# Attention with a small memory, then a gated feed-forward layer: side work at fixed half steps, two output rows fetched in advance, and a last pass that adds on GpSimd and stores on two queues

## The chip, the cores and the metric

The kernel runs on one core of one Trainium2 chip. The metric is the device time of one execution in microseconds. The engines are TensorE (PE, with its weight loads PEld), VectorE (DVE), ScalarE (ACT), GpSimd (POOL) and SyncE (SP); the last three also issue the kernel's DMA transfers.

## The reference, cut to what matters

```python
# attention: B=8, H=8, S=576, D=64, a memory of M=32 slots
a = softmax(phi, axis=2)                            # phi: B,H,S,M
k_m = einsum('bhsm,bhsd->bhmd', a, k)               # keys of the memory
v_m = einsum('bhsm,bhsd->bhmd', a, v)               # values of the memory
attn = softmax(q @ k_m.T / 8)                       # B,H,S,M
x = (attn @ v_m).transpose(0, 2, 1, 3).reshape(4608, 512)
# feed-forward: 512 -> 1536 -> 512
out = (sigmoid(x @ w_gate) * (x @ w_val)) @ w_out
```

## The kernel before

All products are made of a high and a low part in fp32r (hi, lo), three products for each. A batch's attention weights stand turned in at_hi and at_lo. Instead of x, the kernel multiplies the memory's values with the gate's and the value's weights (u_hi, u_lo, made by make_u), so a gate is at times U into pu_t; ScalarE takes the sigmoid of one half (sg or x), VectorE multiplies (L826, L1001), and the parts of the product (g, g_hi, g_lo) go against the output weights into acc.

The program has four stretches. An opening list, written out by hand, ends at about 170 us and is not touched. The **main loop** (to about 391 us) works through batches 0 to 3, four of the twelve blocks of 128 gate columns at a time (TURN): a step is one block, it has two half steps, and after each four steps a batch's sums go to DRAM (part) or, for the last four, to the output. The **second loop** works through batches 4 to 7 with twelve passes (s = 0 to 11) for each batch, where `seven` makes seven products of sums of columns in place of eight (ring holds the weights; acc takes them), and `merge` adds them up into two rows of 128x512. Then comes the tail: the last `seven`, the last `merge`, and the stores.

Beside both loops runs the side work for the batches to come. For phi: its maximum nmx (`a_max`, L420), exp (`a_exp`, which writes ph and its sum z), the turning (T0 to T2), and sums (`memory`). For the scores: `scores`, their maximum (`s_max`, `s_minus`), exp in place in e (`s_exp`), `normalize`, and `turn` into at_hi. Exp and sigmoid need different tables on ScalarE, so an ACT_TABLE_LOAD stands on either side of a stretch of exps. Side work is handed out piece by piece:

```python
            beside = chain(kept_keys(b + 1), softmax(b + 1, then), attend(b + 1), turns_of(then) if then else ())
            slots = iter([1] + [0] * 8 + [1, 0, 1, 0, 1, 0, 1, 0, 1, 1, 1, 1])
```

`go_on` runs once in each half step and takes as many pieces as slots says. Each engine works off its instructions in order. The order of TensorE's products, of the sigmoids and exps, and of the DMA issues of one queue is that of the code; the rest is placed by a scheduler, which may pull an instruction forward. `behind()` holds what is in it back behind the last sigmoid, product, u and conversion that were written before it. The maxima, exps and turns of phi are outside of it before the change.

At the end of four steps `out_end` adds acc to the earlier sum in row (L871) and stores it. `row_of` takes one of two buffers named row and fetches the earlier sum on ScalarE's queue ("rows"); other queues are "batch" on SyncE and "stream" on GpSimd. A batch has four such rows of 128x512. Rows 0 and 1 are fetched when the second half of a step comes to its end, rows 2 and 3 when the first two are stored, since they use the same two buffers. Six rooms named left, of the same size, hold what is left over of gates (the last 64 rows of a batch) until `out_left` works it off.

Of the kernel before, what the change touches and what calls it, by code (L numbers as in the profile page):

```python
# [2 lines left out]

# [17 lines left out]
P = 128  # L21
# [20 lines left out]
DONE = 20  # L42
NBLK = 2
PAIRS = NFT // 2 // NBLK
LEFT_AT = [(1, 2), (0, 0)]
AHEAD = {(1, 0): 2, (0, 1): 2}
SEVEN = [(0, 3, 0), (1, 0, 0), (5, 0, 1), (4, 1, 0), (3, 1, 1), (2, 2, 0), (6, 2, 1)]


# [64 lines left out]
def attn_moe_kernel(  # L114
# [510 lines left out]
    def s_max(b, c=None):  # L625

        e = blocks(b, c)
        w = e.shape[2]
        mx = note("mx")[:, :, :w]
        nc.vector.tensor_reduce(mx, e, axis=AX.X, op=ALU.max)  # L630
        loaded[b, "mx", c] = mx
# [132 lines left out]
        for i, f in enumerate(fs):  # L764
            U[b, f] = (hi[:, :, i], lo[:, :, i])

    left = {}

    def left_of(pair, f):

# [57 lines left out]
    def gate_hi(b, f, c):  # L828
        prod = G[b, f, c][1]
        g = g_tile()  # L830
        ghi, glo = g[:, :, 0], g[:, :, 1]
        nc.scalar.copy(ghi, prod[:, : 2 * P].rearrange("p (j x) -> p j x", j=2))  # L832
        if c:
            if f % TURN == 0 and b % 2 == 0:
                left[b // 2, f // TURN] = ob.tile([P, TURN, P], F32, name="left", bufs=6)
            ls = slice((b % 2) * TAIL, (b % 2) * TAIL + TAIL)
            nc.scalar.copy(left_of(b // 2, f)[:, ls], prod[:, 2 * P :])
        G[b, f, c] = [ghi, glo, prod]
# [6 lines left out]
    def out_half(b, f, c, at_start, at_end):  # L845
        out_of(b, f, c, at_start, at_end)
        if at_end:
            out_end(b, f, c)
        if (b, f + 1) in ends and c:
            for t in range(2):  # L850
                rows[b, t] = row_of(b, t)

    def out_of(b, f, c, at_start, at_end):
# [211 lines left out]
    def merge(b, n, c):  # L1065

        ab, bb, cb, db = acc.pop((b, c))
        r0, r1 = (pools["two"].tile([P, DM], F32, name="row", bufs=2) for _ in range(2))
        q0, q1 = (r.rearrange("p (h x) -> p h x", h=2) for r in (r0, r1))
        nc.scalar.copy(q1[:, 0], db[:, :256])  # L1070
        nc.vector.tensor_tensor(q0, q1[:, 0:1].broadcast_to([P, 2, 256]), ab.rearrange("p (h x) -> p h x", h=2), op=ALU.add)
        nc.vector.tensor_tensor(q1, q0[:, 1:2].broadcast_to([P, 2, 256]), bb.rearrange("p (h x) -> p h x", h=2), op=ALU.add)
        nc.vector.tensor_tensor(q0[:, 1], q1[:, 0], bb[:, 256:], op=ALU.add)
        nc.vector.tensor_tensor(r1, r1, cb, op=ALU.add)
        if n == 0:
            part[b, c] = [dram.tile([P, DM], F32, name=f"part{b}_{c}_{i}") for i in range(2)]
            for d, r in zip(part[b, c], (r0, r1)):
                move(d, r)
            return
        for i, r in enumerate((r0, r1)):  # L1080
            nc.vector.tensor_tensor(r, r, lasting(i), op=ALU.add)
        for r, order in ((q0, (0, 1)), (q1, (1, 0))):
            for t in range(2):
                h = order[t]
                at_row = b * S + (2 * c + t) * P
                move(out[at_row : at_row + P, h * 256 : (h + 1) * 256], r[:, t])

    def part_fetch(b, c):
        for i, d in enumerate(part.pop((b, c))):
# [93 lines left out]
    second = keep.tile([P, NG, S], F32, name="at_hi", bufs=2)  # L1183
    once = note("z")[:, :1]
    step(curve, once, ident[:, :1], AF.Exp)
    rooms.update(dict.fromkeys((1, 2), [ob.tile([P, TURN, P], F32, name="left", bufs=6) for _ in range(NG + 1)]))
    minus = pools["conv"].tile([P, P], F32R, name="minus", bufs=1)
    nc.scalar.activation(minus, ident, AF.Copy, scale=-1.0)
    warm(24)
# [51 lines left out]
    def softmax(b, then=None):  # L1241

        s_max(b)
        s_minus(b)
        yield
        if then is not None:
            a_max(then)
        yield
        s_exp(b)
        if then is not None:  # L1250
            a_exp(then)
        yield

    def attend(b):
        with behind():
            normalize(b)
        yield
        with behind():
            turn(b)
        if b + 1 < B and b + 1 != QUAD:  # L1260
            load_q(b + 1)
        yield

    def turns_of(b):

        for g in range(NG + 1):
            phi_turn(b, g)
            phi_copy(b, g)
            yield

    def memory(b):
        phi_sum(b)
        keys(b)
# [3 lines left out]
    def kept_keys(b):  # L1277
        keys_turn(b)
        keys_keep(b)
        yield  # L1280

    def load_next(b):
        if b < B:
            load_phi(b)
            load_kv(b)

    before_u, sides = {}, {}
    t0 = len(steps)
    before_u[t0 - 13] = lambda: scores(QUAD, 0)
    before_u[t0 - 9] = lambda: scores(QUAD, 1)  # L1290
    before_u[t0 - 1] = lambda: memory(QUAD + 1)
    prepared, pieces = prepare(), iter([1] * 8 + [2, 1] * 6 + [1] * 20)
    sides[begin[2, NFT - TURN]] = ([1] * 8, softmax(QUAD, QUAD + 1))
    sides[begin[3, NFT - TURN]] = ([1] * 8, attend(QUAD), turns_of(QUAD + 1))
# [6 lines left out]
    beside, slots = iter(()), iter(())  # L1301

    def go_on():

        for _ in range(next(slots, 0)):
            next(beside, None)
        if i >= max(CONVERT):
            for _ in range(next(pieces, 0)):
                next(prepared, None)
# [4 lines left out]
    for i, (b, f, at_start, at_end) in enumerate(steps):  # L1314
        if i < DONE:
            continue
        if i in sides:
            run(beside)
            beside, slots = chain(*sides[i][1:]), iter(sides[i][0])
        if i in returns:  # L1320
            again(returns[i])
        if i > max(CONVERT) and (QUAD, "q") not in loaded:
            load_q(QUAD)
        if i == begin[2, 2 * TURN] + 2:
            run(prepared)
# [12 lines left out]
        go_on()
        gate_half(b, f, 1)
        while len(pend) >= LAG:  # L1340
            out_half(*pend.pop(0))
        pend.append((b, f, 1, at_start, at_end))
        if i in u_at:
            if i + 1 == len(steps):
                run(beside)
            if i in before_u:
                before_u[i]()
            make_u(*u_at[i])
            while len(pend) > (1 if i + 1 < len(steps) else 0):
                out_half(*pend.pop(0))  # L1350
        next(extra, None)
        go_on()
        del U[b, f]
    run(out_left(1, 8, 4))
    later.close()
# [9 lines left out]
    held, beside, slots = None, iter(()), iter(())  # L1365
    for i, (b, n, c, k) in enumerate(order):
        s = i % (2 * NBLK * PAIRS)
        more = b + 1 < B
        if s == 0:
            run(beside)  # L1370
            then = b + 2 if b + 2 < B else None
            if more:
                beside = chain(kept_keys(b + 1), softmax(b + 1, then), attend(b + 1), turns_of(then) if then else ())
                slots = iter([1] + [0] * 8 + [1, 0, 1, 0, 1, 0, 1, 0, 1, 1, 1, 1])
            else:
                beside, slots = iter(()), iter(())
# [6 lines left out]
        go_on()  # L1383
# [6 lines left out]
        if more and (n, c, k) == (0, 1, 0):  # L1390
            scores(b + 1, 0)
        if more and (n, c, k) == (0, 0, 1):
            scores(b + 1, 1)
        if more and then and (n, c, k) == (1, 0, 1):
# [10 lines left out]
        held = (now, b, n, c, k)  # L1405
        if b % 2 and (c, k) == LEFT_AT[0]:
            left_parts(b // 2, n)
        go_on()
    seven(*held)

# [52 lines left out]
```

## Time and profile before

| | us |
|---|---|
| median of 3 runs (lowest, highest) | 733.78 (732.91, 736.26) |
| the profiled execution | 733.81 |
| its span, first to last instruction | 732.0 |
| mean granted clock of TensorE, share of full | 0.994 |
| busy: TensorE, VectorE, ScalarE, GpSimd | 708.6, 513.4, 381.5, 35.4 |

The span is that of the one core. Busy time does not count DMA issues and waits. An engine's idle time matters only where the last engine to finish, here TensorE for nearly the whole span, waits for it.

### The profile page before, as it was taken

To read this page: it belongs to the slowest core of one execution; us is meant where nothing else is said; L and a number is where in the kernel's file an instruction comes from. 1 tells how busy PE (TensorE), PEld (TensorE's weight loads), DVE (VectorE), ACT (ScalarE), POOL (GpSimd) and SP (SyncE) were. 2 spreads that over 40 slices of the span, in tenths; PEclk is the share of its full clock that TensorE was granted. 3 is DMA by queue.
4 is the path that set the end of the run, shared out by engine and by line. 5 is a ranking of instruction groups with operands and counts; after the bars stand their busy time and mean duration, and the time that the engine had idled before them with its cause. 6 is when DMAs were issued, how large, how long until landed. Compare 5 with 4: busy or idle time off the path is not lost.

```text
span 732.0 us, 15358 instructions
## 1 busy us (share of the span) xinstructions
PE 708.6 (97%) x6129; PEld 620.2 (85%) x6129; DVE 513.4 (70%) x1050; ACT 381.5 (52%) x878; POOL 35.4 (5%) x71
## 2 busy tenths in 40 slices
PE   8999999999999999999988998999899999999996
PEld 6778888887988887987776988898898989999996
DVE  2899767545676675884536678777777788976766
ACT  5998785555555343345252465444644446544432
POOL 0000000000000012211000000000000000000000
PEclk9999999999999999999999999999999999999999
DMA  8978746464775474768676255781644718381633
GB/s 335 413 274 315 274 156 205 170 238 151 266 247 200 147 250 183 246 244 293 232 292 222 105 209 174 286 335 43 248 174 132 282 50 320 113 308 55 244 123 95
DMA packets 46343, 158.27 MB, mean 216 GB/s; under 512 B 5440, under 2 KB 13632, under 8 KB 41152
## 3 DMA queue, kind: packets, MB, share of 16 engines
q1 hardware_dynamic: 35056, 93.33, 35.4%
q0 software_dynamic: 7184, 56.62, 21.3%
q10 hardware_dynamic: 4032, 7.34, 3.0%
q8 instruction: 48, 0.79, 0.4%
q14 instruction: 23, 0.19, 0.1%
HBM read 118.74 MB, written 38.54 MB: 215 GB/s over the span
## 4 chain that ended last, share of the span: by engine, by line
PE 81%; DMA 8%; DVE 5%; ACT 3%; issue 2%; SPq 0%; POOL 0%; DVEq 0%; ACTq 0%; POOLq 0%
PE pu_t L235 49%; PE acc L235 32%; DMA out_dram<-row 2%; DMA row<-part 2%; DMA block<-kvm 2%; DMA wg<-in_wgv_dram 1%; ACT L210 1%; DVE u_lo L225 1%; ACT ph L210 1%; DMA ph<-in_phiT_dram 1%; DVE row L871 0%; DVE kvm L225 0%; DVE x L1001 0%; SPq L221 0%; ACT u_hi L742 0%
## 5 line engine op out<-in xcount | busy, mean ns | idle before, releaser
L235 PE MATMUL pu_t<-at_hi,u_hi 128*128 128x256 f32 (+1 forms) x760 | 226.0, 297 | 7.7 <-ACT x L210 4.5
L235 PE MATMUL pu_t<-at_hi,u_lo 128*128 128x256 f32 (+1 forms) x760 | 223.2, 294 | 0.0
L235 PE MATMUL pu_t<-at_lo,u_hi 128*128 128x256 f32 (+1 forms) x760 | 223.2, 294 | 0.0
L235 PEld LDWEIGHTS pu_t<-at_hi,u_hi 128*128 128x128 f32 x760 | 143.1, 188 | 15.5 <-ACT x L210 5.3
L235 PEld LDWEIGHTS pu_t<-at_lo,u_hi 128*128 128x128 f32 x760 | 143.2, 188 | 3.0
L235 PEld LDWEIGHTS pu_t<-at_hi,u_lo 128*128 128x128 f32 x760 | 143.2, 188 | 0.0
L235 PE MATMUL acc<-wo_hi,g 128*128 128x512 f32 x384 | 135.7, 399 | 1.7 <-DVE row L871 1.7
L235 PEld LDWEIGHTS acc<-wo_hi,g 128*128 128x128 f32 x384 | 72.1, 188 | 24.2 <-issue 9.2
L210 ACT ACTIVATE sg<-pu_t 128x256 f32<-128x256 f32 x94 | 38.4, 410 | 83.0 <-PE pu_t L235 75.8
L225 DVE TENSOR_TENSOR g_lo<-x,g_hi 128x128 fp32r<-128x128 f32 x144 | 65.8, 463 | 14.6 <-ACT g_hi L1043 12.4
L826 DVE TENSOR_TENSOR sg<-pu_t,sg 128x256 f32<-128x256 f32 (+1 forms) x94 | 42.2, 450 | 47.9 <-ACT sg L210 37.4
L235 PE MATMUL acc<-wo_lo,g 128*128 128x512 f32 x192 | 75.2, 392 | 0.0
L210 ACT ACTIVATE x<-pu_t 128x320 f32<-128x320 f32 (+1 forms) x96 | 39.3, 409 | 66.7 <-PE pu_t L235 66.1
L1001 DVE TENSOR_TENSOR x<-pu_t,x 128x320 f32<-128x320 f32 (+1 forms) x96 | 43.4, 454 | 32.4 <-PE pu_t L235 20.3
L225 DVE TENSOR_TENSOR u_lo<-pu_t,u_hi 128x512 fp32r<-128x512 f32 x92 | 58.1, 681 | 11.1 <-ACT u_hi L742 11.1
L832 ACT CAST g<-sg 128x256 fp32r<-128x256 f32 x96 | 39.0, 406 | 37.3 <-DVE sg L826 30.3
L742 ACT CAST u_hi<-pu_t 128x512 fp32r<-128x512 f32 x92 | 48.7, 592 | 14.6 <-PE pu_t L235 14.1
L235 PE MATMUL pu_t<-wg,vT 64*32 64x512 f32 x736 | 50.5, 598 | 0.1
L225 DVE TENSOR_TENSOR g<-sg,g 128x256 fp32r<-128x256 f32 x96 | 39.5, 418 | 15.5 <-ACT g L832 15.3
L235 PE MATMUL acc<-wo_hi,g_hi 128*128 128x256 f32 x224 | 42.7, 290 | 0.0
L235 PEld LDWEIGHTS acc<-wo_hi,g_hi 128*128 128x128 f32 x224 | 36.0, 197 | 5.9 <-issue 5.9
L235 PE MATMUL acc<-ring,g_hi 128*128 128x256 f32 x224 | 40.5, 281 | 0.0
(194 smaller groups left out, 1145.4 us busy)
## 6 DMA issues: line engine op xcount, KB each, us to landing
kvm<-in_kvm_dram SPq DMA_DIRECT2D x16, 1024.0 KB, 8.3
ring<-block POOLq DMA_DIRECT2D x8, 1792.0 KB, 8.7
wo_hi<-block POOLq DMA_DIRECT2D x7, 1792.0 KB, 7.7
wo_lo<-block POOLq DMA_DIRECT2D x7, 1792.0 KB, 9.2
part<-row SPq DMA_DIRECT2D x48, 256.0 KB, 2.4
q<-in_qT_dram SPq DMA_DIRECT2D x16, 512.0 KB, 5.1
row<-part ACTq DMA_DIRECT2D x28, 256.0 KB, 5.5
block<-kvm POOLq DMA_DIRECT2D x12, 512.0 KB, 4.7
```

What stands on the lines that cost most here:

```text
L210: last_act[0] = nc.scalar.activation(*args, **kw)
L225: return nc.vector.tensor_tensor(lo, x, hi.bitcast(F32), op=ALU.subtract)
L235: last_pe[0] = do(*args, **kw)
L742: nc.scalar.copy(U[b, fs[0]][0][:, r, :nf], pb[r])
L826: last_prod[0] = nc.vector.tensor_tensor(sg, val, sg, op=ALU.mult)
L832: nc.scalar.copy(ghi, prod[:, : 2 * P].rearrange("p (j x) -> p j x", j=2))
L1001: last_prod[0] = nc.vector.tensor_tensor(x[:, :n], val, x[:, :n], op=ALU.mult)
```

## The change

1. Side work has tables of half steps in place of pieces and slots: SIDE_1 in the main loop (counted from the last turn of batch 2), SIDE in the second loop (two for each pass). All of it is inside `behind()`. In the second loop exps of phi (pexp) and of the scores (eexp) have half steps of their own, 3 and 10; before, both stood at 13. The maximum of phi (amax) stands at half step 2, in the main loop at 5, the exps there at 7.
2. The two score blocks of the main loop move from 13 and 9 steps ahead of its end to 17 and 13.
3. `out_half` fetches all four rows of a batch at once, rows 2 and 3 into left rooms. The rooms are named by number (`left_room`).
4. AHEAD has other numbers. In the order of products this puts four sevens instead of two ahead of the scores and of `memory` in pass (0, 1), and nothing else moves.
5. In the last `merge` GpSimd adds the earlier sum to r0, VectorE adds it to r1 before cb, and r1's two stores go out on ScalarE's queue.

```diff
+SIDE_1 = {0: ('max',), 5: ('amax',), 7: ('exp',), 9: ('sum',), 10: ('turn', 'T0'), 14: ('T1', 'T2')}
+PREP = [1] * 8 + [2, 1] * 6 + [1] * 20
+SC_AT = {(0, 1, 0): 0, (0, 0, 1): 1}
+MEMORY_AT = (1, 0, 1)
+SC1_AT = (17, 13)
+SIDE = {0: ('keys',), 2: ('amax',), 3: ('pexp',), 9: ('max',), 10: ('eexp',), 15: ('sum', 'turn'), 18: ('T0',), 20: ('T1', 'T2')}
 LEFT_AT = [(1, 2), (0, 0)]
-AHEAD = {(1, 0): 2, (0, 1): 2}
+AHEAD = {(1, 2): 3, (1, 1): 5, (1, 0): 2, (0, 2): 3, (0, 1): 4, (0, 0): 6}
...
-    left = {}
+    left, left_rooms = {}, []
+
+    def left_room(k):
+        while len(left_rooms) < 6:
+            left_rooms.append(ob.tile([P, TURN, P], F32, name="left", bufs=6))
+        return left_rooms[k]
+
+    SPARE = {k: (1, 2) if k < 7 else (3, 5) for k in range(12)}
+    steps_at = [0]
...
-            for t in range(2):
+            for t in range(SF if (b, 2) in part else 2):
                 rows[b, t] = row_of(b, t)
...
+        if t >= 2 and (b, t) in part:
+            st = left_room(SPARE[steps_at[0] // TURN][t - 2]).rearrange("p f x -> p (f x)")
+            move(st, part[b, t], queue)
+            return st
...
+        last = b == B - 1 and n == NBLK - 1 and c == 0
+        if last:
+            nc.gpsimd.tensor_tensor(r0, r0, lasting(0), op=ALU.add)
+            nc.vector.tensor_tensor(r1, r1, lasting(1), op=ALU.add)
         nc.vector.tensor_tensor(r1, r1, cb, op=ALU.add)
...
-        for i, r in enumerate((r0, r1)):
+        for i, r in enumerate(() if last else (r0, r1)):
             nc.vector.tensor_tensor(r, r, lasting(i), op=ALU.add)
...
-                move(out[at_row : at_row + P, h * 256 : (h + 1) * 256], r[:, t])
+                to = out[at_row : at_row + P, h * 256 : (h + 1) * 256]
+                move(to, r[:, t], "rows" if last and r is q1 else "batch")
...
+    def new_side(b, then):
+
+        work = {"keys": lambda: kept_keys(b), "max": lambda: (s_max(b), s_minus(b)), "eexp": lambda: s_exp(b)}
+        work["sum"], work["turn"], work["next"] = lambda: normalize(b), lambda: turn(b), b + 1
+        work["exp"] = lambda: s_exp(b)
+        if then:
+            work["amax"], work["pexp"] = lambda: a_max(then), lambda: a_exp(then)
+            work["exp"] = lambda: (s_exp(b), a_exp(then))
+            for g in range(NG + 1):
+                work[f"T{g}"] = lambda g=g: (phi_turn(then, g), phi_copy(then, g))
+        return work
+
+    def beside_step(at, k):
+
+        for name in at.get(k, ()):
+            if name in side:
+                with behind():
+                    side[name]()
+                if name == "turn" and side["next"] < B:
+                    load_q(side["next"])
...
-    before_u[t0 - 13] = lambda: scores(QUAD, 0)
-    before_u[t0 - 9] = lambda: scores(QUAD, 1)
+    before_u[t0 - SC1_AT[0]] = lambda: scores(QUAD, 0)
+    before_u[t0 - SC1_AT[1]] = lambda: scores(QUAD, 1)
...
-        go_on()
+        beside_step(SIDE, 2 * s)
...
-        go_on()
+        beside_step(SIDE, 2 * s + 1)
```

**ScalarE, exps of the second loop.** Line numbers are shifted by the change (L210 becomes L216, L1003 L1021, L1039 L1057, L1043 L1061, L742 L748). x and acc carry numbers of buffers; L210 is the helper `curve` for every sigmoid and exp. Before, in batch 4's passes, both exps stand together:

```order
L210 ACTIVATE x_5184<-pu_t 128x320
L210 ACT_TABLE_LOAD
L210 ACTIVATE e<-e 128x1152
L210 ACTIVATE ph,z<-ph,nmx 128x576 x2
L1070 COPY row<-acc_5014 128x256
L1003 COPY vT<-x_5184 128x64
L1039 CAST g_hi<-x_5184 128x2x128
L1043 CAST g_hi<-x_5161 128x512
L742 CAST u_hi<-pu_t 128x512 x2
L210 ACT_TABLE_LOAD
```

Now the exps of ph stand five passes earlier:

```order
L216 ACTIVATE x_4755<-pu_t 128x320
L216 ACT_TABLE_LOAD
L216 ACTIVATE ph,z<-ph,nmx 128x576 x2
L1021 COPY vT<-x_4755 128x64
L1057 CAST g_hi<-x_4755 128x2x128
L1061 CAST g_hi<-x_4730 128x512
L216 ACT_TABLE_LOAD
```

and that of e one pass earlier, between the first and the second sigmoid of a pass:

```order
L216 ACTIVATE x_5080<-pu_t 128x256
L1045 CAST g_hi<-x_5080 128x128
L216 ACT_TABLE_LOAD
L216 ACTIVATE e<-e 128x1152
L216 ACT_TABLE_LOAD
L216 ACTIVATE x_5102<-pu_t 128x256
L216 ACTIVATE x_5146<-pu_t 128x320
```

Each stretch of exps has two table loads of its own; in the whole program there are 20 in place of 16.

**ScalarE, main loop, the turn after batch 2's last one.** DMA rows are the fetches. Before, rows 2 and 3 of batch 2 are fetched into row, four sigmoids apart from any exp:

```order
L742 CAST u_hi<-pu_t 128x512 x4
L210 ACTIVATE sg<-pu_t 128x256
L210 ACTIVATE sg<-pu_t 128x320
L832 CAST g<-sg 128x2x128
L221 DMA row<-part_2_7_3025 128x512
L221 DMA row<-part_3_7_3030 128x512
L210 ACTIVATE sg<-pu_t 128x256
```

Now the exps stand in front of the four casts, and behind the next sigmoid the fetches of the next batch's rows 0 and 1, then in left its rows 2 and 3:

```order
L216 ACTIVATE sg<-pu_t 128x320
L216 ACT_TABLE_LOAD
L216 ACTIVATE e<-e 128x1152
L216 ACTIVATE ph,z<-ph,nmx 128x576 x2
L846 CAST g<-sg 128x2x128
L851 COPY left<-sg 128x64
L748 CAST u_hi<-pu_t 128x512 x4
L216 ACT_TABLE_LOAD
L216 ACTIVATE sg<-pu_t 128x256
L227 DMA row<-part_0_7_3277 128x512
L846 CAST g<-sg 128x2x128
L216 ACTIVATE sg<-pu_t 128x320
```

**VectorE, the maximum of batch 6's phi.** Before, at the end of the main loop:

```order
L225 TENSOR_TENSOR g<-sg,g 128x2x128
L420 TENSOR_REDUCE nmx<-ph 128x2
L225 TENSOR_TENSOR u_lo<-pu_t,u_hi 128x512 x4
L225 TENSOR_TENSOR g<-left,g 128x512
L871 TENSOR_TENSOR row<-acc_4379,row 128x512
```

Now, in the second pass of the second loop (L225 becomes L231, L420 L426, L1001 L1019):

```order
L231 TENSOR_TENSOR g_lo<-x_4638,g_hi 128x512
L231 TENSOR_TENSOR u_lo<-pu_t,u_hi 128x512 x2
L1019 TENSOR_TENSOR x_4730<-pu_t,x_4730 128x320
L426 TENSOR_REDUCE nmx<-ph 128x2
L1046 TENSOR_TENSOR x_4730<-x_4730 128x128
L231 TENSOR_TENSOR g_lo<-x_4730,g_hi 128x128
```

It has moved from in front of u_lo to between the first x of a pass and the difference that is made of it.

## Rows read from the trace of the kernel before

**Rows 1.** The page: busy us (share of the span) and instructions of each engine.

```profile
PE 708.6 (97%) x6129; PEld 620.2 (85%) x6129; DVE 513.4 (70%) x1050; ACT 381.5 (52%) x878; POOL 35.4 (5%) x71
```

**Rows 2.** TensorE's waits, 170 to 720 us: us in all, times, longest.

```profile
PE pu_t L235 <- ACT x L210: 4.5, 2, 2.3
PE acc L235 <- DVE row L871: 1.7, 1, 1.7
PE pu_t L235 <- DVE g L225: 1.4, 1, 1.4
PE pu_t L235 <- DVE u_lo L225: 1.4, 1, 1.4
PE pu_t L235 <- DVE sg L826: 1.3, 2, 1.0
PE pu_t L235 <- DVE x L1001: 1.2, 1, 1.2
PE pu_t L235 <- ACT e L457: 1.0, 1, 1.0
PE pu_t L235 <- ACT x L622: 0.6, 1, 0.6
```

**Rows 3.** Timeline of ScalarE at 432 us: start, length [idle time before].

```profile
433.98 1.28 ACT L210 ACT_TABLE_LOAD   x1
435.27 1.17 ACT L210 ACTIVATE e<-e 128x1152 f32<-128x1152 f32 x1
436.35 0.76 ACT L210 ACTIVATE ph<-ph,nmx 128x576 f32<-128x576 f32 x1
...
440.17 1.28 ACT L210 ACT_TABLE_LOAD   x1
```

**Rows 4.** Window: length; busy PE, PEld, DVE, ACT, POOL; granted clock; DMA share; GB/s.

```profile
440.00:460.00 20.00, 18.05 (x133) 18.05 (x134) 16.69 (x35) 9.49 (x23) 0.00 (x0) 0.91 0.55 192
```

**Rows 5.** Chain of waits, at 400 and at 440 us: start, length, what.

```profile
403.64 2.48 PE acc L235 x21
...
444.70 3.29 PE acc L235 x21
```

**Rows 6.** Timeline of ScalarE at 361 us.

```profile
361.50 0.38 ACT L210 ACTIVATE sg<-pu_t 128x256 f32<-128x256 f32 x1 [5.79 <-PE pu_t L235]
```

**Rows 7.** Chain of waits, 350 to 370 us.

```profile
349.59 3.01 PE acc L235 x12
...
353.34 7.38 DMA out_dram<-row
```

**Rows 8.** Timeline of ScalarE, 343 to 350 us.

```profile
345.53 0.44 ACT L210 ACTIVATE sg<-pu_t 128x320 f32<-128x320 f32 x1 [0.98 <-PE pu_t L235]
...
348.83 2.06 ACT L742 CAST u_hi<-pu_t 128x512 fp32r<-128x512 f32 x4 [1.33 <-PE pu_t L235]
```

**Rows 9.** Timeline of VectorE, 384 to 397 us.

```profile
384.01 1.35 DVE L420 TENSOR_REDUCE nmx<-ph 128x2 f32<-128x1152 f32 x1 [4.95 <-DMA ph<-in_phiT_dram]
385.28 2.47 DVE L225 TENSOR_TENSOR u_lo<-pu_t,u_hi 128x512 fp32r<-128x512 f32 x4
...
395.12 1.37 DVE L871 TENSOR_TENSOR row<-acc,row 128x512 f32<-128x512 f32 x2 [3.41 <-DMA row<-part]
```

**Rows 10.** Timeline of ScalarE at 614 us.

```profile
614.38 1.28 ACT L210 ACT_TABLE_LOAD   x1 [0.25 <-PE pu_t L235]
```

**Rows 11.** Timeline of VectorE and of SyncE's queue, from 725 us.

```profile
725.82 0.42 DVE L1073 TENSOR_TENSOR row<-row,acc 128x256 f32<-128x256 f32 x1
...
727.55 0.69 DVE L1081 TENSOR_TENSOR row<-row,wo_lo 128x512 f32<-128x512 f32 x1
...
727.66 1.80 SPq L221 DMA_DIRECT2D out_dram<-row  x4
```

**Rows 12.** DMA issues: count, KB each, median us from issue to landing.

```profile
out_dram<-row SPq DMA_DIRECT2D x16, 256.0 KB, 2.8
```

**Rows 13.** GpSimd's groups: busy us, mean ns, idle us before.

```profile
masks.py:199 POOL TENSOR_SCALAR_AFFINE_SELECT ident<-ident 128x128 f32<-128x128 f32 x1 | 0.3, 287 | 0.1
```

More of the change, by code (lines that the diff above doesn't have):

```diff
@@ L1 @@
 from contextlib import ExitStack, contextmanager
-from itertools import chain, cycle
+from itertools import cycle
 import concourse.bass as bass
@@ L834, in gate_hi @@
             if f % TURN == 0 and b % 2 == 0:
-                left[b // 2, f // TURN] = ob.tile([P, TURN, P], F32, name="left", bufs=6)
+                left[b // 2, f // TURN] = left_room((NG + 1 + f // TURN * 2 + b // 2) % 6)
             ls = slice((b % 2) * TAIL, (b % 2) * TAIL + TAIL)
@@ L1185, in attn_moe_kernel @@
     step(curve, once, ident[:, :1], AF.Exp)
-    rooms.update(dict.fromkeys((1, 2), [ob.tile([P, TURN, P], F32, name="left", bufs=6) for _ in range(NG + 1)]))
+    rooms.update(dict.fromkeys((1, 2), [left_room(k) for k in range(NG + 1)]))
     minus = pools["conv"].tile([P, P], F32R, name="minus", bufs=1)
@@ L1239, in attn_moe_kernel @@
         ACTIONS[name](*map(int, args)) if name == "W" else step(ACTIONS[name], *map(int, args))
[L1241 to L1269, printed above, removed]
     def memory(b):
@@ L1285, in load_next @@
             load_kv(b)
-    before_u, sides = {}, {}
+    before_u = {}
     t0 = len(steps)
-    before_u[t0 - 13] = lambda: scores(QUAD, 0)
-    before_u[t0 - 9] = lambda: scores(QUAD, 1)
+    before_u[t0 - SC1_AT[0]] = lambda: scores(QUAD, 0)
+    before_u[t0 - SC1_AT[1]] = lambda: scores(QUAD, 1)
     before_u[t0 - 1] = lambda: memory(QUAD + 1)
-    prepared, pieces = prepare(), iter([1] * 8 + [2, 1] * 6 + [1] * 20)
-    sides[begin[2, NFT - TURN]] = ([1] * 8, softmax(QUAD, QUAD + 1))
-    sides[begin[3, NFT - TURN]] = ([1] * 8, attend(QUAD), turns_of(QUAD + 1))
+    prepared, pieces = prepare(), iter(PREP)
     returns = {
@@ L1299, in attn_moe_kernel, with go_on @@
     lefts = {begin[2, TURN] + 6: (0, 0, 8), begin[0, 2 * TURN] + 2: (1, 0, 8), begin[2, 2 * TURN] + 2: (0, 8, 4)}
[L1301 to L1306, printed above, removed]
+    side = new_side(QUAD, QUAD + 1)
+    def go_on(half):
+        beside_step(SIDE_1, 2 * (i - begin[2, 2 * TURN]) + half)
         if i >= max(CONVERT):
@@ L1316, in attn_moe_kernel @@
             continue
-        if i in sides:
-            run(beside)
-            beside, slots = chain(*sides[i][1:]), iter(sides[i][0])
+        steps_at[0] = i
         if i in returns:
@@ L1337, in attn_moe_kernel @@
         pend.append((b, f, 0, at_start, at_end))
-        go_on()
+        go_on(0)
         gate_half(b, f, 1)
@@ L1343, in attn_moe_kernel @@
         if i in u_at:
-            if i + 1 == len(steps):
-                run(beside)
             if i in before_u:
@@ L1351, in attn_moe_kernel @@
         next(extra, None)
-        go_on()
+        go_on(1)
         del U[b, f]
@@ L1364, in attn_moe_kernel @@
     order = [(b, n, c, k) for b in range(QUAD, B) for n in range(NBLK) for c in (1, 0) for k in range(PAIRS)]
-    held, beside, slots = None, iter(()), iter(())
+    held, side = None, {}
     for i, (b, n, c, k) in enumerate(order):
@@ L1369, in attn_moe_kernel @@
         if s == 0:
-            run(beside)
             then = b + 2 if b + 2 < B else None
[L1372 to L1376, printed above, removed]
+            side = new_side(b + 1, then) if more else {}
         if b % 2 and s % (2 * PAIRS) == 0:
@@ L1382, in attn_moe_kernel @@
         first_half(b, f, c)
-        go_on()
+        beside_step(SIDE, 2 * s)
         now = second_half(b, f, c, k)
@@ L1389, in attn_moe_kernel @@
             seven(*held, SEVEN[:ahead])
[L1390 to L1394, printed above, removed]
+        if more and (n, c, k) in SC_AT:
+            scores(b + 1, SC_AT[n, c, k])
+        if more and then and (n, c, k) == MEMORY_AT:
             memory(then)
@@ L1407, in attn_moe_kernel @@
             left_parts(b // 2, n)
-        go_on()
+        beside_step(SIDE, 2 * s + 1)
     seven(*held)
```

1 line of the change is left out of this document (removed).

## The prediction, made before the changed kernel was run

> **What bounds the kernel now.** I read the page's engine table first. TensorE is busy 708.6 us, 97% of a span of 732.0 [rows 1]. The products themselves are the same before and after the change, so only TensorE's idle time, its clock and the two ends can give anything. The next view is TensorE's list of waits, from 170 us on, where the part that the diff touches begins: 4.5 (2 times) + 1.7 + 1.4 + 1.4 + 1.3 (2 times) + 1.2 + 1.0 + 0.6 = 13.1 us in ten waits [rows 2]. I then looked up each place on the engine that TensorE waited for. There are four kinds.
>
> *The exps beside the second loop.* TensorE waits twice, the longest 2.3 us, for the gate's sigmoid (x, L210). ScalarE's timeline shows why: between two table loads (433.98 and 440.17, 1.28 each) stand an exp of 1.17 and two of 0.76, with copies behind them, and the sigmoid starts only after the second load [rows 3]. After such a wait the granted clock is lower: 0.91 over the 20 us around it [rows 4], as of 3.6 us at half, 1.2 of 2.4 GHz, and 9% of 20 us is 1.8 us lost. The chain shows the same loss in its pieces: 21 acc products that take 2.48 us at 403 take 3.29 there [rows 5]. Batches 4 and 5 have one such place each; the second repeats the first.
>
> *The exps in the main loop.* At 332 us a row add (L871) held TensorE's acc, 1.7 us [rows 2]: on VectorE it is queued behind z (L462), which needs the exp of ph.
>
> *A row fetch on ScalarE's queue.* At 355 to 361.5 us ScalarE did nothing for 5.79 us [rows 6]. The timeline calls the releaser PE, but the chain shows the real one: the store out_dram<-row took 7.38 us, and the fetch row<-part into the same buffer, which stands on ScalarE's queue in front of that sigmoid, had to wait for it [rows 7]. TensorE paid 1.3 + 1.0 = 2.3 us. At 395 us it is the same chain of store and fetch: VectorE's row adds waited 3.41 us for row<-part, the gate's product behind them came late, and TensorE paid 1.2 and then 0.6 [rows 2, 9].
>
> *The maximum of phi.* nmx (L420) stands on VectorE in front of u_lo, and its queue stands 4.95 us for phi's load [rows 9]. TensorE paid 1.4 for g behind it, and 1.4 for u_lo at a second place of the same form in batch 4.
>
> **The change, part by part.** *Exps, second loop.* The first wait (half step 13) is split: ph at half step 3, e at 10. Together they hold ScalarE for 2 x 1.28 + 1.17 + 1.52 = 5.25 us and cost TensorE 4.5 / 2 = 2.25, so about 3.0 us were covered. The e exp alone holds 2 x 1.28 + 1.17 = 3.73. The trace has it alone already, in batch 6, where no phi follows (at 609 us): behind its second load ScalarE has even been idle 0.25 us, waiting for TensorE [rows 10], and none of TensorE's ten waits lies there. So 3.7 us were covered, and e alone costs nothing, three times. The ph exps alone hold 2 x 1.28 + 1.52 = 4.08. By the cover of 3.0 that is 1.1 a time, by the cover of 3.7 0.4. By the order, copies that TensorE needs stand between exp and second load, as in batch 6, so I take 0.5, twice: 1.0 (bounds 0 and 2.2). Gain: 4.5 of waits and 2 x 1.8 = 3.6 of clock.
>
> On this the Trainium skill speaks against the change: "ScalarE: Activation LUTs", Rules for kernel authors, says to group by table set and do all of one set before switching, and counts about 2.7 us a switch, of which 1.28 is the load. The load agrees with the trace's 1.28 [rows 3]; no idle time of 1.4 beside it is seen there, since the exp starts 1.29 after the load started. By the trace the four more loads cost ScalarE 4 x 1.28 = 5.1 us, by the page 4 x 2.7 = 10.8, and if TensorE had to wait for all of it, the time would be up by as much; whether TensorE sees them decides.
>
> *Exps and maximum, main loop.* They move to about 346 us, between a sigmoid that ends at 345.53 + 0.44 = 345.97 and four casts u_hi that began at 348.83 [rows 8]. One load and the exps end at 345.97 + 1.28 + 1.17 + 1.52 = 349.9, two small copies follow, and u_hi begins 1.8 late, at about 350.6. The gate needs the first u_hi and u_lo, 0.52 (2.06 / 4) and about 0.6 (2.47 / 4), so at 351.8; TensorE has 12 acc products until 349.59 + 3.01 = 352.6 [rows 7 to 9]. The cover holds by 0.8, and I count the 1.7 as gained; with the cover gone it is the 1.8 that u_hi is late.
>
> *Maximum of phi.* Batch 6's moves from 384 us, in front of u_lo, to behind the first x of the second loop's second pass, past 400 us: the load has landed by 384.0 [rows 9], so no wait is left. Batch 7's moves alike. 1.4 + 1.4 gained. Its own 1.35 now stands between x and the copies of a gate; the 21 acc products of the pass before, 2.5 us [rows 5], lie over it. Taken at nothing; without the cover it is 1.35 a place.
>
> *Rows in advance.* Rows 2 and 3 (the third and fourth) go to left rooms that are idle, so their fetch no longer waits for the store of rows 0 and 1: 1.2 + 0.6 gained. Not all fetches are free of it, though: in the new order ScalarE issues row<-part for the next batch's rows 0 and 1 directly behind the first sigmoid after the exps, and that buffer has just been stored. The store took 7.38 behind a load of a weight block on SyncE's queue; the median for such a store is 2.8 [rows 7, 12]. With the median the hold is 5.79 - (7.38 - 2.8) = 1.2 us, and as it begins about 1 us earlier, 2 us. TensorE lost 2.3 of 5.79, so 3.5 was covered: 2 us costs nothing. Gain 2.3, bounds 0 and 2.3.
>
> *Scores and the sevens ahead.* The main loop's two score blocks move four steps earlier, and two more sevens stand before scores and memory in the second loop. The same products stand elsewhere on TensorE, their operands ready by many us; nothing.
>
> *The tail.* From 725.82 to 727.55 VectorE begins four adds, 0.58 apart, and SyncE issues four stores from 727.66 on, 1.80 / 4 = 0.45 each [rows 11]. One add goes to GpSimd, so VectorE ends 0.58 earlier; r1's two stores go out on ScalarE's queue from about 727.65, r0's two on SyncE's when GpSimd is done. The last store is then issued 2 x 0.45 = 0.9 earlier. The trace has no GpSimd add; its nearest row is a select over 128x128 in 0.287, by four for 128x512 1.15 [rows 13]. From 725.82 + 0.42 = 726.24 it ends at 727.4, earlier than needed. Lower bound as VectorE's 0.69; upper bound twice 1.15 for two operands, 728.5, which takes the whole 0.9 away. I take 0.9.
>
> The Trainium skill gives the same add on GpSimd as 1.96 times VectorE's ("GPSIMD Engine Reference", Elementwise). By that page it would end at 726.24 + 1.96 x 0.69 = 727.6 and the tail would gain 0.9 all the same.
>
> **The sum.** Gains 13.1 + 3.6 + 0.9 = 17.6; new waits 1.0; net 16.6. The profiled execution took 733.81 (span 732.0 and 1.8 around it), the median of the runs is 733.78. So 733.8 - 16.6 = 717.2 us. With the new wait at nothing it is 716.2.
>
> **The rivals.** *The fetch still holds ScalarE* at 354 us, as long as now. The 2.3 of rows 2 stay, and if it comes in one piece, the clock falls as it did at the other waits over 2 us, 1.8 more: 717.2 + 4.1 = 721.3. For it speaks that the store still stands behind a load on SyncE's queue; against it, that the load is issued earlier, since the last cast that makes its weights no longer stands behind the exps.
>
> *The split puts table loads on TensorE's path.* With half of each hold uncovered that is 2 x 2.04 + 3 x 1.87 = 9.7, and with the clock fallen after the two ph exps, as after the waits of 2.25, 13.3 in place of 1.0: 729.5. With a quarter uncovered and no fall of the clock it is 2 x 1.02 + 3 x 0.93 = 4.8, so 721.0. For it speaks that four more loads stand between sigmoids, against it batch 6. It is the way that the skill's rule of grouping would have it go.
>
> *Slower:* ScalarE stands in front of gates at every one of five exps, with nothing covered. Then TensorE loses 3 x 3.73 + 2 x 4.08 = 19.4, and with a clock loss of 1.8 at five places 28.4: 733.8 - 17.6 + 28.4 = 744.6. It decides from (17.6 / 5) = 3.5 us for each exp on, that is 1.7 of idle time with the clock's 1.8. Against it: the same kind of place at 609 us cost nothing.
>
> *The waits only move:* TensorE comes earlier to the next product, and the load or add behind it is as late as before, so that three quarters come back: 729 to 733. Against it: DMA and VectorE have room in most of these stretches, and the waits are of single places, not of a rate.
>
> **Chances.** Mine 0.55 (its own range 715 to 720); the fetch 0.17; the table loads 0.15; moved waits 0.08; slower 0.05. Half a per cent, 3.7 us, is about what a measurement of this kernel can tell from no change. Faster than 730.1: the first three but for the edge of the third, and a part of the fourth, 0.88; within it 0.08; slower 0.04. The range goes from 714.5 (some small wait that I did not list gone too) to 726, which takes in the fetch and most of the table loads and leaves out about 0.2.
>
> **What would show it.** In the list of waits no wait of TensorE for x (L210 by its new line) over 1 us, and the granted clock at 1.00 at 440 to 460 and 520 to 540: right on the split. A piece DMA out_dram<-row in the chain near 350 us: the fetch. VectorE's nmx with no idle time before it: right on the maximum. In the tail a GpSimd add under 1.4 us and a last store issued 0.9 earlier after the last product. Wrong would be a wait of over 2 us at half step 3 or 10 of a batch, with the clock at half behind it.

## The result and the profile after

The changed kernel takes 714.37 us (median of 4 runs, 713.92 to 715.72), the kernel before beside it 734.25 (732.91 to 736.26). The ratio is 0.973, 95% interval 0.9703 to 0.9757: faster by 2.7%. Forecast were 717.2 us and a range from 714.5 to 726, so the time lies 0.13 us below the range's lower end. The profiled execution took 713.92 with a span of 712.1, 19.9 us less than before.

The page's engine table, and shares of the chain that ended last:

```profile
PE 700.1 (98%) x6129; PEld 616.6 (87%) x6129; DVE 510.7 (72%) x1049; ACT 386.8 (54%) x882; POOL 37.1 (5%) x72
...
PE 95%; DVE 2%; DMA 1%; ACT 0%; POOLq 0%; issue 0%; SPq 0%; POOL 0%; DVEq 0%
```

TensorE is busy 8.5 us less than in [rows 1], with the same 6129 products. "Busy" holds products at the lower clock and short waits inside of blocks, so the gain is not all idle time. The list of waits of [rows 2], for 170 to 712 us, is empty; it has its heading alone:

```profile
core 0 of [0], span 712.1 us
engine line waited for: us in total, times, longest us
```

The windows in which the waits for x stood, now at 420 and 500 us (columns as in [rows 4]), have the clock at 1.00, the upper level, in place of 0.91:

```profile
420.00:440.00 20.00, 20.00 (x162) 19.03 (x161) 18.34 (x40) 11.32 (x30) 0.58 (x2) 1.00 0.75 259
500.00:520.00 20.00, 20.00 (x162) 19.03 (x161) 16.61 (x37) 11.75 (x27) 1.05 (x2) 1.00 0.84 306
```

ScalarE's timeline shows the two stretches of exps that took the place of [rows 3]: those of ph at 392 us, of e at 417, each between two loads:

```profile
392.02 1.28 ACT L216 ACT_TABLE_LOAD   x1
393.32 0.78 ACT L216 ACTIVATE ph<-ph,nmx 128x576 f32<-128x576 f32 x1
...
395.93 1.28 ACT L216 ACT_TABLE_LOAD   x1
...
416.91 1.28 ACT L216 ACT_TABLE_LOAD   x1
418.20 1.17 ACT L216 ACTIVATE e<-e 128x1152 f32<-128x1152 f32 x1
419.39 1.28 ACT L216 ACT_TABLE_LOAD   x1
```

VectorE now takes the maximum of batch 6's phi with no idle time before it, where it had 4.95 [rows 9] (its timeline):

```profile
391.11 1.34 DVE L426 TENSOR_REDUCE nmx<-ph 128x2 f32<-128x1152 f32 x1
```

The fetch of rows 0 and 1 still waits for a store, but 1.70 us in place of the 5.79 of [rows 6] (ScalarE's timeline):

```profile
353.69 0.33 ACTq L227 DMA_DIRECT2D row<-part  x1
354.06 0.41 ACT L846 CAST g<-sg 128x256 fp32r<-128x256 f32 x1 [1.70 <-DMA out_dram<-row]
```

**Where the time came from.** The products of u stand in the same order in both programs, so their starts in the two timelines cut the program into comparable stretches. Two of these pairs, before and then after:

```profile
175.48 1.09 PE L235 MATMUL pu_t<-wg,vT 64*32 64x512 f32 x16
...
610.43 1.09 PE L235 MATMUL pu_t<-wg,vT 64*32 64x512 f32 x16
```

```profile
174.41 1.09 PE L241 MATMUL pu_t<-wg,vT 64*32 64x512 f32 x16
...
588.64 1.09 PE L241 MATMUL pu_t<-wg,vT 64*32 64x512 f32 x16
```

| stretch, us of before | before | after | less by | waits and clock counted there |
|---|---|---|---|---|
| 0 to 175.48 | 175.48 | 174.41 | 1.1 | 0 |
| to 347.65 | 172.17 | 169.83 | 2.3 | 1.7 |
| to 380.09 | 32.44 | 29.17 | 3.3 | 2.3 |
| to 434.94 | 54.85 | 49.96 | 4.9 | 3.2 |
| to 523.53 | 88.59 | 82.73 | 5.9 | 5.45 |
| to 610.43 | 86.90 | 82.54 | 4.4 | 4.05 |
| to 724.32, the last merge's first add | 113.89 | 113.57 | 0.3 | 0 |
| to the end, 732.04 | 7.72 | 9.93 | -2.2 | 0.9 |

Two things stand out: every stretch gave more than its waits, 21.0 against 16.7 in the middle, and the tail is longer.

The tail first. The timeline shows the adds and stores, the view of the program's last line the drains (count, then ns shortest, median and longest, first and last start), and the chain the last piece:

```profile
702.21 0.69 DVE L1089 TENSOR_TENSOR row<-row,acc 128x512 f32<-128x512 f32 x1 [0.54 <-PE acc L241]
...
704.27 1.71 POOL L1094 TENSOR_TENSOR row<-row,wo_hi 128x512 f32<-128x512 f32 x1 [34.10 <-DVE row L1091]
...
705.72 0.87 ACTq L227 DMA_DIRECT2D out_dram<-row  x2
706.00 0.84 SPq L227 DMA_DIRECT2D out_dram<-row  x2
...
L1458 POOLq DRAIN  x3: 40/93/7139, 704.2 to 711.9; - x3
...
704.24 1.74 POOLq L1458
```

GpSimd's add takes 1.71 us and ends at 705.98. Behind it stands a drain that was begun at 704.24 and lasted 7.14, so to 711.38; the end of the program waits for it. The last stores were issued by 706.84 and land 2 us later.

### The profile page after: what moved, and what is told of

It reads as the page before. It is cut to its first block, busy times and chain, and to the rows that moved or that the text cites. A ratio compares the mean times of both kernels' runs of the same rounds, so it can differ in the third digit from the quotient of the medians.

```text
span 712.1 us, 15370 instructions
## 1 busy us (share of the span) xinstructions
PE 700.1 (98%) x6129; PEld 616.6 (87%) x6129; DVE 510.7 (72%) x1049; ACT 386.8 (54%) x882; POOL 37.1 (5%) x72
## 4 chain that ended last, share of the span: by engine, by line
PE 95%; DVE 2%; DMA 1%; ACT 0%; POOLq 0%; issue 0%; SPq 0%; POOL 0%; DVEq 0%
PE pu_t L241 58%; PE acc L241 37%; DMA wg<-in_wgv_dram 1%; POOLq L1458 0%; DVE e L666 0%; DVE zs L658 0%; DVE g_lo L231 0%; DVE wg L345 0%; ACT wg L260 0%; ACT wg L261 0%; DVE e L589 0%; DVE mx L582 0%; SPq L227 0%; DVE wg L340 0%; DVE row L1089 0%
## 5 line engine op out<-in xcount | busy, mean ns | idle before, releaser
L216 ACT ACTIVATE sg<-pu_t 128x256 f32<-128x256 f32 x94 | 38.5, 410 | 84.4 <-PE pu_t L241 77.4
L231 DVE TENSOR_TENSOR g_lo<-x,g_hi 128x128 fp32r<-128x128 f32 x144 | 66.3, 465 | 11.5 <-ACT g_hi L1061 10.7
L216 ACT ACTIVATE x<-pu_t 128x320 f32<-128x320 f32 (+1 forms) x96 | 39.1, 410 | 59.6 <-PE pu_t L241 59.1
L231 DVE TENSOR_TENSOR u_lo<-pu_t,u_hi 128x512 fp32r<-128x512 f32 x92 | 57.9, 682 | 14.6 <-ACT u_hi L748 14.6
L1019 DVE TENSOR_TENSOR x<-pu_t,x 128x320 f32<-128x320 f32 (+1 forms) x96 | 43.4, 453 | 32.7 <-ACT x L216 20.9
L748 ACT CAST u_hi<-pu_t 128x512 fp32r<-128x512 f32 x92 | 48.6, 592 | 13.8 <-PE pu_t L241 12.9
L231 DVE TENSOR_TENSOR g<-sg,g 128x256 fp32r<-128x256 f32 x96 | 39.4, 418 | 16.0 <-ACT g L846 15.8
L1061 ACT CAST g_hi<-x 128x512 fp32r<-128x512 f32 x48 | 29.7, 619 | 24.7 <-DVE x L1059 24.6
L241 PE MATMUL acc<-wo_hi,g_hi 128*128 128x256 f32 x224 | 41.0, 282 | 0.0
```

The source lines that it names most:

```text
L216: last_act[0] = nc.scalar.activation(*args, **kw)
L231: return nc.vector.tensor_tensor(lo, x, hi.bitcast(F32), op=ALU.subtract)
L241: last_pe[0] = do(*args, **kw)
L748: nc.scalar.copy(U[b, fs[0]][0][:, r, :nf], pb[r])
L1019: last_prod[0] = nc.vector.tensor_tensor(x[:, :n], val, x[:, :n], op=ALU.mult)
L1061: nc.scalar.copy(gh[:, 2:6], x[:, 1:5])
```

## Experiments

All start from the changed kernel. A profile's span is split in three: to the first product of u after 170 us (opening), from there to the first add of the last merge (middle), and from there to the end (tail). The opening is the same code in all and lasted 174.4 to 177.4 us. In it TensorE waits for loads that come earlier or later (for q up to 2.7 us, in the run with one column on GpSimd), and in the three longest openings (176.4 to 177.4) the granted clock was 0.91 or 0.92 from 20 to 40 us, where the changed kernel has 1.00. So I compare middles and tails.

| run | opening | middle | tail | span |
|---|---|---|---|---|
| kernel before | 175.5 | 548.8 | 7.7 | 732.0 |
| changed kernel | 174.4 | 527.8 | 9.9 | 712.1 |
| changed kernel again | 174.5 | 527.4 | 9.95 | 711.9 |
| old tail | 175.2 | 528.4 | 7.7 | 711.4 |
| both adds on VectorE, two queues | 174.6 | 527.6 | 7.6 | 709.8 |
| GpSimd's add one merge earlier | 174.5 | 527.3 | 7.7 | 709.5 |
| halves on two queues | 176.7 | 528.9 | 7.5 | 713.2 |
| one column on GpSimd | 177.4 | 528.2 | 7.6 | 713.2 |
| exps together at 13 | 175.6 | 532.7 | 9.95 | 718.2 |
| exps together at 10 | 175.0 | 530.5 | 9.95 | 715.5 |
| rows late | 174.9 | 534.1 | 9.95 | 718.9 |
| main loop's exps early | 175.1 | 531.1 | 9.95 | 716.2 |
| scores late | 174.4 | 528.1 | 9.95 | 712.5 |
| maximum pulled forward | 176.4 | 536.8 | 9.95 | 723.1 |

Where the middle was not touched it is 527.3 to 528.9, 527.8 in the median of seven profiles. Where it was touched there is one profile each, so a change of the middle under about 1 us says little by itself.

### The tail: what GpSimd's add costs

```diff
-        last = b == B - 1 and n == NBLK - 1 and c == 0
-        if last:
-            nc.gpsimd.tensor_tensor(r0, r0, lasting(0), op=ALU.add)
-            nc.vector.tensor_tensor(r1, r1, lasting(1), op=ALU.add)
+        last = False
```

> The changed kernel with the tail as before: r0 and r1 added on VectorE, all four last stores on SyncE. In the trace of the changed kernel GpSimd's drain, behind its add, ends 5.4 us after that add and is what the end waits for. If that is the cause, the span falls by 2.2 us, from 712.1 to about 709.9, and the time from 714.4 to about 712.2. If the drain is only an onlooker and the tail's gain of 0.9 us is real, the span grows by 0.9 us, to 713.0.

The tail is 7.7, as before the change: 2.2 us less. The span fell by 0.8 only, since opening and middle were 1.4 longer here. Time 712.78 us (5 runs), ratio 0.9712 (0.9699 to 0.9725).

```diff
-            nc.gpsimd.tensor_tensor(r0, r0, lasting(0), op=ALU.add)
+            nc.vector.tensor_tensor(r0, r0, lasting(0), op=ALU.add)
```

> The changed kernel with r0's last add on VectorE instead of GpSimd; the two queues for the last stores stay. If GpSimd's drain is the price: span about 709.7 us, a little under the run with the whole old tail, since the last store is issued about 0.3 us earlier. If the two queues are what lengthens the tail: span about 712.1, as in the changed kernel.

Span 709.8, tail 7.6; time 711.74 (4 runs), ratio 0.971 (0.969 to 0.9729). So the two queues alone gain 0.15 us, not 0.9, and GpSimd's add costs 2.35.

```diff
+            add = nc.gpsimd if b == B - 1 and i == 0 else nc.vector
-            nc.vector.tensor_tensor(r, r, lasting(i), op=ALU.add)
+            add.tensor_tensor(r, r, lasting(i), op=ALU.add)
```

> As the run before, but GpSimd adds r0 in the last merge but one, some 20 us ahead of the end. If GpSimd pays for its drain once, whenever it has computed something, the drain at the end takes over 5 us again and the span is near 712. If the price is only that the drain begins so late, nothing of it is seen at the end: span about 709.7.

This takes the last merge's adds from the run before, both on VectorE, and has GpSimd add r0 of the merge ahead of it. Tail 7.7. Its GpSimd add and the drain behind it:

```profile
L1104 POOL TENSOR_TENSOR row<-row,wo_hi 128x512 f32<-128x512 f32 x1 | 1.3, 1293 | 22.4 <-DVE row L1091 22.4
...
L1459 POOLq DRAIN  x3: 40/102/6726, 692.1 to 709.2; - x3
```

The drain lasts again, 6.73 us, of which the add is 1.29; but it begins at 692.1 and is over 10 us before the end. The price is the drain's place.

```diff
+            nc.gpsimd.tensor_tensor(r0[:, :1], r0[:, :1], lasting(0)[:, :1], op=ALU.add)
+            nc.vector.tensor_tensor(r0[:, 1:], r0[:, 1:], lasting(0)[:, 1:], op=ALU.add)
-            nc.gpsimd.tensor_tensor(r0, r0, lasting(0), op=ALU.add)
```

> The changed kernel with r0's last add split: GpSimd adds one column of 512, VectorE the other 511. If what lengthens the tail is a drain of fixed length behind GpSimd's last instruction (5.4 us behind the add of 1.71 us): from the first add of the last merge to the end 2.1 us to the add, some 0.3 us for it, 5.4 us and 0.7 us for the end, 8.4 us, in place of 9.9. If the drain grows with the work behind it: 7.6 to 7.7, as with the add on VectorE.

```profile
706.36 0.19 POOL L1094 TENSOR_TENSOR row<-row,wo_hi 128x1 f32<-128x1 f32 x1 [32.81 <-DVE row L1089]
...
L1459 POOLq DRAIN  x3: 40/102/5632, 706.3 to 712.9; - x3
```

The add of one column takes 0.19 and ends at 706.55; the drain ends at 706.31 + 5.63 = 711.94, 5.4 us behind it. Behind the add of 512 columns it was 711.38 - 705.98 = 5.4 too. The drain does have a fixed length behind the last instruction, as the first theory has it; my sum for the tail was wrong, because one column is ready behind the first add of the merge already, so that the drain was over before the stores had landed.

```diff
-                move(to, r[:, t], "rows" if last and r is q1 else "batch")
+                move(to, r[:, t], "rows" if last and t else "batch")
```

> Both last adds on VectorE, and of each row one half is stored on SyncE's queue and one on ScalarE's, so that the last store is issued with the first half of its row: 0.4 us earlier than with r1's two halves one behind the other on ScalarE. If the issue of the stores sets the end: span 709.4, time about 711.3. If their landing does (they land 1.6 to 2.0 us after the issue, the later the more go at once): no gain over that run, 709.8.

Both adds on VectorE here too. Tail 7.5: no gain worth the name over 7.6. Time 713.58 (4 runs, 711.46 to 714.94), ratio 0.9715 (0.9692 to 0.9739); its profile has the second longest opening of all.

> The changed kernel once more, on the chip and beside the runs of the kernel before of this call. If GpSimd's add costs 2.2 us at the end, it is 2.2 to 2.6 us above the run with the halves on two queues; if not, both are within 0.5 us.

714.42 us (5 runs), ratio 0.9739 (0.9716 to 0.9763), 0.8 above the halves measured beside it, and not 2.2. In the two profiles the tail is 9.95 against 7.5, but the halves have an opening 2.2 and a middle 1.5 longer. The other runs have no profile, so it is not shown that openings hide the tail in the medians too.

### The exps of the second loop

```diff
-SIDE = {0: ('keys',), 2: ('amax',), 3: ('pexp',), 9: ('max',), 10: ('eexp',), 15: ...
+SIDE = {0: ('keys',), 2: ('amax',), 9: ('max',), 13: ('eexp', 'pexp'), 15: ...
```

> The changed kernel with both exps of the second loop together at half step 13 again. If the split is what frees TensorE: two waits of about 2.25 us for x in batches 4 and 5 and 1.8 us of clock behind each, so span 712.1 + 8.1 = about 720. If it is rather that the side work is held back behind the gate's sigmoids (the place on ScalarE): no such waits, span about 712.

TensorE's waits from 170 us on:

```profile
PE pu_t L241 <- DVE u_lo L231: 3.5, 3, 1.4
```

Three waits of 1.4 at most, the clock at 1.00 in the windows of the first two (420 to 440 and 510 to 530 us), middle up by 4.9: between the two theories. The third wait is in batch 6, where e's exp stands alone and where it cost nothing before the change [rows 10]. So the order in which the other work stands around the exps counts as well as their length. It also means that the split is not the whole of the gain. In the stretch that ends at 610.43 us before the change, where the list had nothing but the exps' wait and its clock, this run takes 594.05 - 509.36 = 84.7 us: it gives back 2.1 of the 4.4. The rest came with something else in the change that no run here undoes alone: the holding back of the side work other than the maximum, or part 4, the sevens ahead.

```diff
+SIDE = {0: ('keys',), 2: ('amax',), 9: ('max',), 10: ('eexp', 'pexp'), 15: ...
```

> The changed kernel with both exps of the second loop together at half step 10. If it is the length of the hold that counts (5.25 us in place of 3.73, of which the place covers about 3.7): waits of TensorE of up to 1.5 us in batches 4 and 5, span up by 2 to 3.5 us. If it is the place alone: no wait, span as in the changed kernel but for the first 22 us, which differ from run to run by up to 1 us.

```profile
PE pu_t L241 <- ACT x L216: 2.2, 2, 1.1
```

Two waits of 1.1, middle up by 2.7, as the length of the hold has it: of 5.25 us some 4.1 are covered at half step 10. By these two profiles the split is worth 2.7 us there, the place (10, not 13) another 2.2.

### Rows in advance, and the hold of ScalarE's queue

```diff
-            for t in range(SF if (b, 2) in part else 2):
+            for t in range(2):
...
-        if t >= 2 and (b, t) in part:
+        if False:
```

> The changed kernel without the rows in advance: rows 2 and 3 are fetched into the two row buffers when rows 0 and 1 are stored, as before. If the fetch in advance frees both places (ScalarE's hold near 355 us and the row adds near 395 us): TensorE's waits of 2.3 and 1.8 us come back, span up by 4 to 6 us. If the hold near 355 us had gone with the exps and the earlier load of the weight block: only the 1.8 us come back, up by 2 us.

```profile
PE pu_t L241 <- ACT x L216: 2.2, 1, 2.2
PE pu_t L241 <- issue: 1.9, 1, 1.9
```

Both waits are at the start of the second loop. The first is for a sigmoid: ScalarE's queue stood 10.76 us behind the two late fetches, which waited for the store. The second has no releaser in the list; there VectorE's row adds wait for the same fetches. The timelines of ScalarE and VectorE and the window of that place:

```profile
387.91 0.44 ACT L216 ACTIVATE x<-pu_t 128x320 f32<-128x320 f32 x1 [10.76 <-DMA out_dram<-row]
...
389.66 1.30 DVE L885 TENSOR_TENSOR row<-acc,row 128x512 f32<-128x512 f32 x2 [5.86 <-DMA row<-part]
...
380.00:400.00 20.00, 15.89 (x108) 12.54 (x107) 9.59 (x21) 6.77 (x17) 0.54 (x1) 0.83 0.67 226
```

Middle up by 6.3: the waits are 4.1, not the 1.8 of before, and the clock, at 0.83, makes up the rest. No wait came back near 355 us. So the fetch in advance freed the second place alone, on both engines, and undone in the finished kernel it costs much more there than I had for it.

```diff
-SIDE_1 = {0: ('max',), 5: ('amax',), 7: ('exp',), 9: ...
+SIDE_1 = {0: ('max',), 1: ('amax',), 2: ('exp',), 9: ...
```

> The changed kernel with the main loop's exps and maximum back at half steps 2 and 1, all of it still held back behind the gates. If the place is what cost 1.7 us: a wait of 1 to 2 us near 330 us, span up by 1.7 to 2. If the row add behind z was the scheduler's doing: no wait, span unchanged.

```profile
PE pu_t L241 <- DVE sg L840: 1.6, 1, 1.6
PE pu_t L241 <- ACT sg L216: 1.3, 1, 1.3
...
360.58 0.41 ACT L846 CAST g<-sg 128x256 fp32r<-128x256 f32 x1 [6.03 <-DMA out_dram<-row]
```

Middle up by 3.3. The 1.3 is the exps' own (at 335 us). The 1.6 stands behind a hold of ScalarE by the fetch of 6.03 us: with the exps early, the old hold of 5.79 [rows 6] is back. So it was the place of the exps and the maximum, which this run moves together, that shortened it, not the rows in advance. SyncE's timelines show how: the load of a weight block is issued 7.4 us ahead of the row stores (350.62) in the changed kernel and 2.7 us ahead of them (351.48) here. The stores then land in 3.0 us (median) there, and in 7.8 here. Changed kernel, then this run:

```profile
343.20 0.58 SPq L227 DMA_DIRECT2D wo_hi<-block  x1
...
348.76 0.59 SPq L227 DMA_DIRECT2D wo_hi<-block  x1
```

### The maximum of phi

```diff
-                with behind():
+                with ExitStack() if name == "amax" else behind():
```

> The changed kernel with the maximum of phi not held back behind the gates: in the order of VectorE's instructions nmx of batches 6 and 7 is again pulled forward in front of the four u_lo. If that place, and not the half step in the table, made the two waits of 1.4 us: they come back, span up by about 3 us. If TensorE's other gains have moved the load of phi clear of it: no wait.

```profile
PE pu_t L241 <- DVE u_lo L231: 3.4, 1, 3.4
PE pu_t L241 <- DVE g L231: 1.7, 1, 1.7
...
380.13 1.35 DVE L426 TENSOR_REDUCE nmx<-ph 128x2 f32<-128x1152 f32 x1 [6.58 <-DMA ph<-in_phiT_dram]
```

The place is the cause, and the price has grown: VectorE waits 6.58 for phi's load where it was 4.95 [rows 9]. By the start of the maximum the load has landed 3.9 us earlier than before the change (380.13 against 384.01), but VectorE comes to it 5.5 us earlier (373.55 against 379.06). Two waits of 5.1 us together, the clock at 0.91 behind both (380 to 400 and 450 to 470 us, 2 x 1.8), and the middle is up by 9.0 in place of the 2.8 that stood in my sum.

### Scores

```diff
-SC1_AT = (17, 13)
+SC1_AT = (13, 9)
```

> The changed kernel with the two score blocks 13 and 9 steps ahead of the main loop's end, as before. My prediction had this at nothing. In the traces the products of scores and of u together take 0.57 + 2.47 = 3.0 us before and 0.57 + 2.01 = 2.6 us after: so up by about 0.5 us if the place matters; 0 by the prediction.

The block of scores and u in the timeline of the changed kernel, then with the scores late:

```profile
288.87 0.78 PE L241 MATMUL pu_t<-q,kT 64*32 64x256 f32 x32
289.44 2.08 PE L241 MATMUL pu_t<-wg,vT 64*32 64x512 f32 x32
291.45 0.50 PE L241 MATMUL acc<-wo_hi,g 128*128 128x512 f32 x1
```

```profile
314.83 0.78 PE L241 MATMUL pu_t<-q,kT 64*32 64x256 f32 x32
315.40 2.75 PE L241 MATMUL pu_t<-wg,vT 64*32 64x512 f32 x32
318.08 0.51 PE L241 MATMUL acc<-wo_hi,g 128*128 128x512 f32 x1
```

The block takes 318.08 - 314.83 = 3.25 us in place of 2.58: 0.7 lost, with no wait in the list. The middle is up by 0.3, within its scatter. The one stretch tells more: from the first product of u to that at 344 us it takes 170.45 us, and 169.83 or 169.84 in nine of the ten other profiles that leave this stretch as it is in the changed kernel (170.57 with the halves, which have a wait of 0.5 in it). So the place of the scores is worth 0.6 there, about what that stretch gave above its listed 1.7.

## Why the prediction was wrong

**Waits and clock, second loop: right in kind.** The four more table loads did not reach TensorE. The Trainium skill's rule of grouping ("ScalarE: Activation LUTs", Rules for kernel authors) would have had the exps stay together; here, with the loads at 1.28 and the hold in two pieces, apart was better by 2.7 us at the same half step. Waits and clock came back as counted, 5.9 and 4.4 in the two stretches against 5.45 and 4.05. But I put all of it down to the split, and with the exps together at 13 again the clock did not fall and only about half came back.

**New wait for the ph exps, 1.0: not there.** The cover that I took from other places, 3.0 to 3.7, did not hold at half step 3, where all of the 4.08 was covered. How much of a hold is covered changes with the place: 4.1 us at half step 10, by my count 3.0 at 13 before the change.

**The main loop's exps, 1.7, and the maximum, 2.8: right.** Undone, the exps and their maximum cost 1.5 us in the stretch to 347.65, and the maximum of phi brings both of its waits back.

**The sum of waits, 13.1: too small.** This is the step that failed. I took the list of waits as all that could be had. The list counts from the modelled end of a product to the start of the next. But products that follow without a stop start before that end: in the timeline of TensorE before, at the first wait for x, two products start 0.14 us apart, each listed at 0.31 us.

```profile
439.24 0.31 PE L235 MATMUL pu_t<-at_lo,u_hi 128*128 128x320 f32 x1
439.38 0.31 PE L235 MATMUL pu_t<-at_hi,u_lo 128*128 128x320 f32 x1
441.95 0.42 PE L235 MATMUL pu_t<-at_hi,u_hi 128*128 128x320 f32 x1 [2.26 <-ACT x L210]
```

So the product that waits starts 441.95 - 439.38 = 2.57 us after the last one in place of about 0.15: 2.4 lost, 2.26 listed. Taken from start to start in this way, against the median of the same two products in sequence, the ten waits are 14.9 us and not 13.1, so 1.9 more. The list also leaves out short stops inside a block of products. Where it has 1.2 + 0.6 for the start of the second loop, scores and u took, from their first product to the next gate's, 399.85 - 395.14 = 4.7 us before (first fence) and 388.29 - 386.49 = 1.8 after (second), by the timelines of TensorE:

```profile
395.14 0.62 PE L235 MATMUL pu_t<-q,kT 64*32 64x256 f32 x2
...
399.85 0.42 PE L235 MATMUL pu_t<-at_hi,u_hi 128*128 128x320 f32 x1 [0.62 <-ACT x L622]
```

```profile
386.49 0.66 PE L241 MATMUL pu_t<-q,kT 64*32 64x256 f32 x16
...
388.29 0.41 PE L241 MATMUL pu_t<-at_hi,u_hi 128*128 128x320 f32 x1
```

That is 2.9 in place of 1.8, of which 0.4 is in the 1.9 already, so 0.7 more. Over the middle it is 21.0 in place of 16.7, 4.3 more: 1.9 beside the ten waits, 0.7 in this block, and 0.6 with the scores, which I had at nothing. What is left, about 1.1, I did not take apart. The two more sevens ahead, also at nothing, were not undone alone, so their share is open.

**The tail, 0.9 gained: wrong in sign.** The add took 1.71 us, within my bounds of 0.69 to 2.3. The Trainium skill gives 1.96 times VectorE's time, for 2048 columns ("GPSIMD Engine Reference", Elementwise); against VectorE's 0.69 it was 2.5 times here, and 1.9 in the merge before (1.29 us). But the bound of my sum was the stores, and the end waits for GpSimd's drain, 5.4 us behind its last instruction. The tail lost 2.2.

**Rows in advance, main loop.** The reasoning that the hold at 355 us would shrink from 5.79 to about 2 was right (1.70), by the earlier load and exps, as the early exps show. The second place was mis-sized: 1.8 in my sum, 6.3 when it is undone alone in the finished kernel. That is not what it gained, since the whole stretch gave 4.9.

**Sum and range.** Measured against the terms: 21.0 for 15.7 in the middle, -2.2 for 0.9 in the tail, and 1.1 in the opening, which differs from run to run. The first two errors had opposite signs, 5.3 and -3.1, and it is luck that the time came so near to the range; it still fell below it, since the lower end allowed only 1.7 us for what the list did not show. Without the tail's mistake the medians are 711.7 to 713.6 us (the runs with both adds on VectorE, 711.74 and 713.58, and with the old tail, 712.78). Their intervals overlap with the changed kernel's; what tells them apart is the tail in the profile, 7.5 to 7.7 against 9.9.

## What to carry to other kernels

Where one engine is nearly always busy, size a removed wait by the time between two products that stand on either side of it, with the same pair undisturbed elsewhere beside it, and not by the idle time alone; ask also whether the clock is lower behind it. Undo one part in the finished version before its worth is named: a wait on a load can grow as the rest gets faster (4.95 to 6.58 us for phi). Work given to an idle engine near the end of a program is paid with that engine's own way out, so look at the drains as well as the stores.

## What was not expected of the hardware

- GpSimd's drain ends 5.4 us behind its last computing instruction, whether that takes 1.71 or 0.19 us; with the add one merge earlier 6.73 - 1.29 = 5.4 again.
- GpSimd's add of 128x512 took 1.71 us in the last merge and 1.29 in the merge before it; VectorE's takes 0.69 in both kernels.
- Two stores issued at once on two queues land no earlier than one behind the other: the tail is 7.5 and 7.6 us.
- The opening, the same code in all, lasted from 174.4 to 177.4 us, the three longest with the granted clock at 0.91 or 0.92 from 20 to 40 us.
